# Order of the first loads, the token weight in three tiles, and the order of the first token products in a fused attention and mixer kernel

## Chip, cores and metric

The kernel runs on one core of one Trainium2 chip. The metric is the device time of one execution in microseconds (us); the median of several runs counts.

## What is computed

An attention block without softmax, normalised per head, is followed by an MLP mixer over tokens and then over channels. B = 8 batches, H = 8 heads, S = 576 tokens, D = 64, so d_model = 512; the token hidden size is 256, the channel hidden size 1536. All is float32.

```python
kv = np.einsum('bhsd,bhse->bhde', k, v)
out = np.einsum('bhsd,bhde->bhse', q, kv)
rms = np.sqrt(np.mean(out * out, axis=-1, keepdims=True) + 1e-06)
x = (out / rms * g_norm)            # (B,H,S,D) -> (B, S, H*D)
xt = x.transpose(0, 2, 1)
h = np.maximum(xt @ w_tok1, 0.0) @ w_tok2
u = x + h.transpose(0, 2, 1)
h2 = np.maximum(u @ w_ch1, 0.0) @ w_ch2
return u + h2
```

The four mixer weights arrive as 64-bit floats; the kernel reads them as pairs of 32-bit words and rounds them to 32-bit floats itself.

## The kernel before

Attention and token mixing go over the batches in pairs; the channel mixing of all batches follows and takes most of the time. The change is in the first pair and in the first third of the second ("the start" and "the middle").

**Loads.** `load(n)` (lines 138 to 147) fetches half the heads of one batch's k and v: for each, a DMA for tokens 0 to 511 and one for the last 64. The halves are numbered 0 to 15, and four tiles of each kind are used in turn. k goes on the SP queue, v too, except that v of halves 0 and 1 goes on ACT's queue. `load_q(b)` (149) fetches one batch's q without its last 64 tokens (1 MB), `load_q_rest` these. `block` (189) makes five steps for a part of a weight: step 0 fetches the raw words, step 1 (ScalarE, two instructions: the scaled value into the weight's tile, and the low word in place), step 2 (VectorE, clamp), step 3 (VectorE, shift), step 4 (VectorE, add of the low word). `get_tok1(t)` (204) is for half t of the first token weight, tokens 0 to 511, `get_tok1_rem` (210) for its last 64 tokens, `get_tok2(t)` (214) for the second token weight. The first token weight is one tile `w_tok1` [128, 5, 256] (101). The order of the first fetches is written out from line 1212 on; POOL there only sets padding rows and the identity.

**Order of the rest.** It is written out by hand as lists of step names (`start`, `middle`, `steady`, from line 1242), which `play` (1193) calls one by one. Every engine runs its own instructions in the order in which they are issued (`keep`, 118), and waits for the data. The names, for the first pair: `kv<s><h>` multiplies k and v of batch side s, half h, and `e<s><h>` copies the product out of PSUM (VectorE for side 0 of the first pair, ScalarE else). `a<c><t>` multiplies q with it for token tile c, half t (`a40`: the last 64 tokens of both sides). `g` (VectorE) multiplies with the gain, `q` (ScalarE) squares, `t` (VectorE) sums the squares, `m` (VectorE), `r` (ScalarE) and `i` (VectorE, four instructions) turn a tile's sums into factors. The factor is applied by ScalarE (`s<c><t>`, eight instructions) or by VectorE (`d<c><t>`, one). Tile c of side 0 is 0 or 1, of side 1 is 2 or 3, so the x tiles 0 to 7 are (c, t) in order. `h<s><t>` multiplies weight half t with the four x tiles of side s, `h<s><t><j>` with one of them; `hr` adds the last 64 tokens and takes the relu; `z` and `u` are the second token product. `w<n><k>` is step k of token weight part n (0 and 1 the halves of the first weight, 2 its last 64 tokens, 3 and 4 the second weight). `l`, `lq` and `lr` issue the next loads of k with v, q, and q's rest; `f` fetches a raw channel weight. `j<n>` (`keep_warm`, 1277) is n products of the identity with itself that nothing reads.

PSUM has two banks for attention (`o`), two for the k/v products (`kv`) and four for token products and junk (`h`).

Of the kernel before, what the change touches and what calls it, by code (L numbers as in the profile page):

```python
# [11 lines left out]
F32 = mybir.dt.float32  # L12
# [8 lines left out]
def kernel(  # L21
# [33 lines left out]
    P = 128  # L55
# [3 lines left out]
    DTOK = moe_w_tok1.shape[1]  # L59
    DCH = moe_w_ch1.shape[1]  # L60
    J, JJ, HF = 4, 5, 64
    LO = P * J
    assert D == 64 and DM == 512 and S == LO + HF and B % 2 == 0
    NC, NF, NTOK = DM // P, DCH // P, DTOK // P
# [13 lines left out]
    def pool(name, bufs, side="left", stack=ctx, **kw):  # L78
        return stack.enter_context(tc.tile_pool(name=name, bufs=bufs, side=side,
                                                reuse_waits="tile", **kw))  # L80
# [6 lines left out]
    tokw = pool("tokw", 1, "right", right)  # L87
# [10 lines left out]

    ident = inp.tile([P, P], F32, name="ident")
    g_sb = inp.tile([P, 1, D], F32, name="g_sb")  # L100
    w_tok1 = tokw.tile([P, JJ, DTOK], F32, name="w_tok1")
    w_tok2 = tokw.tile([P, NTOK, S], F32, name="w_tok2")

    w_ch1 = w1p.tile([P, 4, 4, FQ], F32, name="w_ch1")
# [7 lines left out]
    def do(f, *a, **kw):  # L112
        return lambda: f(*a, **kw)
# [6 lines left out]
    def dma(o, i, engine=nc.sync):  # L120
        keep(engine.dma_start(o, i))

    def tensor_add(o, a, b, op=ALU.add, engine=nc.vector):
        keep(engine.tensor_tensor(out=o, in0=a, in1=b, op=op))  # L124

    def relu(o, a):
        keep(nc.scalar.activation(o, a, AF.Relu))  # L127

    def copy(o, a):
        keep(nc.scalar.copy(o, a))  # L130

    def matmul(*a, **kw):
        keep(nc.tensor.matmul(*a, **kw))  # L133
# [4 lines left out]
    def load(n):  # L138

        if n >= 2 * B:  # L140
            return
        cols = [t[n // 2, :, ts(n % 2, DH)] for t in (k, v)]

        queues = (nc.sync, nc.scalar if n < 2 else nc.sync)
        for dst, c, e in zip((k_in[n % 4], v_in[n % 4]), cols, queues):
            dma(dst[:, :J], c[:LO].rearrange("(j p) e -> p j e", p=P), e)
            dma(dst[:HF, J], c[LO:], e)

    def load_q(b):
        if b < B:  # L150
            qT[b] = qtp.tile([P, HP, LO], F32, name="qT", tag="qT", bufs=2)
            dma(qT[b], q[b].rearrange("(c p) s -> p c s", p=P)[..., :LO])
# [29 lines left out]
    def words(w):  # L182
        return w.bitcast(U32).rearrange("r (n w) -> r n w", w=2)
# [5 lines left out]
    def block(n, loads, dst):  # L189

        raw = []

        def fetch():
            raw.append(stage.tile([P, n, 2], U32, name="raw", tag="raw", bufs=4))
            for o, i in loads(raw[0]):
                dma(o, i)

        def turn():
            t = raw[0]
            return t if len(dst.shape) == 2 else t.rearrange("p (a n) w -> p a n w", a=dst.shape[1])  # L200

        return (fetch,) + decode(dst, turn, lambda: raw[0])

    def get_tok1(t):

        rows = words(moe_w_tok1)[:LO].rearrange("(j p) n w -> p j n w", p=P)
        return block(J * P, lambda raw: [(raw.rearrange("p (j n) w -> p j n w", j=J),
                                          rows[:, :, ts(t, P)])], w_tok1[:, :J, ts(t, P)])

    def get_tok1_rem():  # L210
        w = words(moe_w_tok1)[LO:]
        return block(DTOK, lambda raw: [(raw[:HF], w), (raw[HF:], w)], w_tok1[:, J])

    def get_tok2(t):
        return block(S, lambda raw: [(raw, words(moe_w_tok2)[ts(t, P)])], w_tok2[:, t])
# [36 lines left out]
    def t_sums(b):  # L252

        def step(o, x, y):
            return lambda: tensor_add(b(o), b(x), b(y), ALU.subtract)

        return [step(5, 7, 1), step(6, 3, 5), step(7, 3, 7), step(4, 2, 6)]
# [92 lines left out]
    def x_of(pair, i):  # L350

        return X[pair, i // 2][:, i % 2]
# [177 lines left out]
    def token_mixing(pair, seeds, aside=()):  # L530
        h1, acc = {}, {}

        def tok1(side, t, js=range(J)):
            if js[0] == 0:
                acc[side, t] = ps["h"].tile([P, DM], F32, name="ps_h", tag="h")
            for j in js:
                matmul(acc[side, t], lhsT=w_tok1[:, j, ts(t, P)],
                                 rhs=x_of(pair, side * J + j), start=(j == 0), stop=False)

        def tok1_rem():  # L540
            for t in range(NTOK):
                for side in range(2):
                    r = ds(side * HF, HF)
                    matmul(acc[side, t], lhsT=w_tok1[r, J, ts(t, P)],
                                     rhs=x_of(pair, 8)[r], start=False, stop=True)
            for side in range(2):
                h1[side] = hp_.tile([P, NTOK, DM], F32, name="h1", tag="h1")
                for t in range(NTOK):
                    relu(h1[side][:, t], acc[side, t])

        def seed(i):


            acc[i] = ps["h"].tile([P, DM], F32, name="ps_u", tag="h")
            copy(acc[i], x_of(pair, i))

        def tok2(i):
            if i not in seeds:
                n = "o" if i in aside else "h"
                acc[i] = ps[n].tile([P, DM], F32, name="ps_u", tag=n)  # L560
            first = i not in seeds
            if i < 8:
                for t in range(NTOK):
                    matmul(acc[i], lhsT=w_tok2[:, t, ts(i % J, P)], rhs=h1[i // J][:, t],
                           start=(first and t == 0), stop=(t == NTOK - 1), skip_group_check=True)
            else:
                for t in range(NTOK):
                    for side in range(2):
                        matmul(acc[i][ds(side * HF, HF)], lhsT=w_tok2[:, t, LO:],
                               rhs=h1[side][:, t],  # L570
                               start=(first and t == 0), stop=(t == NTOK - 1), skip_group_check=True)
            x = x_of(pair, i)
            if first:
                tensor_add(x, acc[i], x)
            else:
                copy(x, acc[i])
            if i == 8:
                dma(u_rest[ts(pair, P)], x, nc.gpsimd)
                for side in range(2):
                    dma(out[2 * pair + side, LO:], x[ds(side * HF, HF)], nc.gpsimd)  # L580
            elif i % 2 == 1:
                dma(
                    u_rows(2 * pair + i // J)[ds((i % J - 1) * P, 2 * P)]
                    .rearrange("(t p) e -> p t e", p=P), X[pair, i // 2], nc.gpsimd)

        steps = {f"h{s}{t}": do(tok1, s, t) for s in range(2) for t in range(NTOK)}
        steps |= {f"h0{t}{j}": do(tok1, 0, t, (j,)) for t in range(NTOK) for j in range(J)}
        steps |= {f"z{i}": do(seed, i) for i in seeds}
        return steps | {"hr": tok1_rem} | {f"u{i}": do(tok2, i) for i in range(9)}

# [602 lines left out]
    def play(lines, after={}, **stages):  # L1193
# [3 lines left out]
        for name in " ".join(lines).split():  # L1197
# [5 lines left out]
            else:  # L1203
                next(stages[s][name] for s in ("attention", "mixing", "more")
                     if name in stages.get(s, ()))()


    tok1 = [get_tok1(t) for t in range(NTOK)] + [get_tok1_rem()]
    tok2 = [get_tok2(t) for t in range(NTOK)]
    channel = ([get_ch1(c, f) for f in range(2) for c in range(NC)]  # L1210
               + [get_ch2(f) for f in range(NF // 2)])
    load(0)
    for block in tok1[:2]:
        block[0]()
    load(1)
    for t in [t for pair in zip(k_in, v_in) for t in pair]:
        keep(nc.gpsimd.memset(t[HF:, J], 0.0))
    zeroed = [ps["kv"].tile([P, 2, P], F32, name="ps_kv", tag="kv") for _ in range(2)]
    for t in zeroed:
# [5 lines left out]
    make_identity(nc, ident)  # L1225
    dma(g_sb, bass.AP(tensor=g_norm.tensor, offset=g_norm.offset,
                      ap=[[0, P], [0, 1], list(g_norm.ap[0])]), nc.scalar)
    load_q(0)
    for n in range(2, 4):
        load(n)  # L1230
    load_q(1)
# [2 lines left out]
    for block in tok1[2:] + tok2:  # L1234
# [5 lines left out]


    start = [
        "kv00 e00 l00 j14 w01 w11 w02 w03 w04 w12 w13 w14", "kv01 j10 e01 l01",
        "a00 g00 q00", "a01 g01 q01 t00 t01 m0", "a10 q10 r0 i0 d00 d01", "a11 q11 g10 g11 t10",
        "kv10 e10 t11 m1 r1", "h000 h010 h001", "kv11 e11 i1 d10 s11", "h011", "a20 q20",
        "a21 q21 g20 g21 t20 t21 m2", "h002 h012 r2 i2 d20", "a30 q30 g30", "a31 q31 s21 g31 t30", "h003 h013 t31 m3",
        "a40 q40 r3 i3 d30 s31 g40 t40 m4 r4 w21 i4 s40 lq0 l10 l11 lr0 lr1"]
    middle = [
        "kv00 e00 w31 w22 w23 w24", "h10 -lq1 w32 w33 w34", "h11 w41 w42 w43 w44", "kv01 e01", "hr l00 z2",
        "a0 q00 g01 q01 g00 t00 t01", "u0 l01 f0", "u1 z4", "u2", "a1 q10 g11 q11 g10",  # L1250
        "kv10 kv11 e10 e11 t10 t11 m0 r0 lq0", "u3 z6 i0 d00 s01 d11 f1", "u4 l10", "a2 q20 g21 q21 g20",
        "a4 q40 t20 g41 q41 t21 g40 lr0 lr1", "u5 s10 t40 t41 m2 r2 f2 1", "u6 1 i2 p20 p21 l11 x00", "u7 1 1"]
# [17 lines left out]
    more = {f"w{n}{k}": f for n, b in enumerate(tok1 + tok2) for k, f in enumerate(b)}  # L1270
# [6 lines left out]
    def keep_warm(n):  # L1277

        o = ps["h"].tile([P, DM], F32, name="ps_j", tag="h")
        for _ in range(n):  # L1280
            matmul(o[:, :P], lhsT=ident, rhs=ident, start=True, stop=True)

    more |= {f"j{n}": do(keep_warm, n) for n in (10, 14)}
    play(start, attention=attentions[0], mixing=mixings[0], more=more)
    play(middle, attention=attentions[1], mixing=mixings[0], before=attentions[0],
         more=more, rounding=rounding)
    for n in range(1, B // 2 - 1):
        play(steady[n - 1], attention=attentions[n + 1], mixing=mixings[n], before=attentions[n] | {"u8": mixings[n - 1]["u8"]},
             more=more, rounding=rounding)
# [16 lines left out]
    more = {f"c{i}": f for i, f in enumerate(t_sums(lambda n: uT[0][:, SB[n]]))}  # L1306
# [97 lines left out]
```

## Time and profile before

| | us |
|---|---|
| median of 3 runs | 783.54 (783.22 to 783.66) |
| the profiled execution | 783.41 |
| its span, first to last instruction | 781.6 |
| TensorE busy in the span | 769.3 (98%) |
| VectorE busy | 617.4 (79%) |
| ScalarE busy | 271.1 (35%) |
| GpSimd busy | 70.5 (9%) |
| DMA, mean over the span | 246 GB/s |

The span is read from the start of the first instruction to the end of the last. PE is TensorE, DVE VectorE, ACT ScalarE, POOL GpSimd, and SP the engine that issues most DMAs. Matmuls run in a pipeline, so a busy TensorE is not one at its peak; a float32 product is two instructions in the trace. In a row of the timeline stand its start, its length, the engine and line, the operation with its tiles, the shape, the number of instructions, and in brackets the idle time ahead of it with what ended it. That releaser is inferred from semaphores: where an instruction waits for several things, it can be the wrong one.

### The profile page before, as it was taken

The numbers are of one execution on the slowest core, as the hardware profiler recorded it, in microseconds if no ns is written. First come the engines' busy times: TensorE is split into PE (matmuls) and PEld (weight loads), VectorE is DVE, ScalarE is ACT, GpSimd is POOL, SyncE is SP. The second block draws the span as 40 slices with busy tenths as digits, with TensorE's granted clock in tenths as the row PEclk, the third lists the DMA queues.
The fourth block names the chain that finished last, engine by engine and source line by source line (L and its number), as shares of the span: only waits on it lengthen the run. The fifth ranks groups of instructions, "written<-read, shape, count | busy, mean of one in ns | idle before, by whom it ended". The sixth has DMA issues, their size and how long they took to land.

```text
span 781.6 us, 14842 instructions
## 1 busy us (share of the span) xinstructions
PE 769.3 (98%) x5816; PEld 650.6 (83%) x5816; DVE 617.4 (79%) x924; ACT 271.1 (35%) x534; POOL 70.5 (9%) x84
## 2 busy tenths in 40 slices
PE   6999999999999999999999999999999999999998
PEld 5655555545888888999988899998889999889998
DVE  2867887897767779898768888876898885787977
ACT  2576565664210232511144241123352114325211
POOL 1002020113410000010100001010000101000111
PEclk9999999999999999999999999999999999999999
DMA  9999999599699795698996579889559889645864
GB/s 296 322 326 375 361 360 346 199 301 355 252 281 342 267 315 145 178 291 231 221 262 202 159 235 250 249 203 287 158 151 300 197 221 236 198 145 159 197 169 92
DMA packets 132613, 192.12 MB, mean 246 GB/s; under 512 B 13632, under 2 KB 92224, under 8 KB 132544
## 3 DMA queue, kind: packets, MB, share of 16 engines
q1 hardware_dynamic: 115984, 167.54, 68.1%
q0 software_dynamic: 14656, 22.02, 13.7%
q10 hardware_dynamic: 1904, 1.61, 0.7%
q8 instruction: 46, 0.75, 0.4%
q14 instruction: 23, 0.19, 0.1%
HBM read 138.31 MB, written 52.82 MB: 245 GB/s over the span
## 4 chain that ended last, share of the span: by engine, by line
PE 96%; DVE 1%; DMA 1%; ACT 1%; SPq 0%; issue 0%; ACTq 0%
PE ps_d L133 28%; PE ps_b L133 19%; PE ps_a L133 19%; PE ps_u L133 8%; PE ps_h L133 7%; PE ps_v L133 5%; PE ps_c L133 3%; PE ps_o L133 2%; PE ps_kv L133 2%; PE ps_w L133 2%; DMA raw<-in_moe_w_tok_dram 1%; DVE x L445 0%; PE ps_j L133 0%; DVE ms L466 0%; ACT x L499 0%; ACT sq L449 0%
## 5 line engine op out<-in xcount | busy, mean ns | idle before, releaser
L133 PE MATMUL ps_d<-ui,w 128*128 128x256 f32 x504 | 118.7, 379 | 0.0
L130 ACT COPY ps_d<-ps_a 128x768 f32<-128x768 f32 (+1 forms) x56 | 32.0, 571 | 215.3 <-PE ps_a L133 215.3
L133 PEld LDWEIGHTS ps_d<-ui,w 128*128 128x128 f32 x504 | 95.1, 190 | 12.9 <-DVE v L124 0.3
L124 DVE TENSOR_TENSOR v<-v,v 128x1536 f32<-128x1536 f32 (+2 forms) x70 | 103.4, 1482 | 0.3
L133 PE MATMUL ps_b<-w,sv 128*128 128x128 f32 x672 | 84.6, 276 | 0.0
L133 PE MATMUL ps_a<-w,v 128*128 128x128 f32 x672 | 84.2, 275 | 0.0
L133 PEld LDWEIGHTS ps_a<-w,v 128*128 128x128 f32 x672 | 79.8, 192 | 0.2
L133 PEld LDWEIGHTS ps_b<-w,sv 128*128 128x128 f32 x672 | 79.5, 192 | 0.2
L133 PE MATMUL ps_d<-w,v 128*128 128x128 f32 x528 | 66.2, 275 | 0.0
L133 PE MATMUL ps_h<-x,w_tok 128*128 128x512 f32 (+1 forms) x160 | 65.4, 603 | 0.6 <-DVE x L503 0.4
L133 PE MATMUL ps_u<-h,w_tok 128*128 128x512 f32 (+1 forms) x160 | 64.7, 599 | 0.0
L133 PEld LDWEIGHTS ps_d<-w,v 128*128 128x128 f32 x528 | 62.7, 192 | 0.3
L127 ACT ACTIVATE v<-v 128x768 f32<-128x768 f32 (+1 forms) x54 | 42.6, 821 | 55.1 <-DVE v L124 55.1
L133 PE MATMUL ps_d<-w,sv 128*128 128x128 f32 x480 | 60.1, 275 | 0.0
L133 PEld LDWEIGHTS ps_d<-w,sv 128*128 128x128 f32 x480 | 57.1, 192 | 0.2
L133 PEld LDWEIGHTS ps_h<-x,w_tok 128*128 128x128 f32 (+1 forms) x160 | 26.2, 189 | 32.3 <-issue 27.8
L133 PEld LDWEIGHTS ps_u<-h,w_tok 128*128 128x128 f32 (+1 forms) x160 | 25.6, 179 | 31.1 <-issue 26.7
L1122 POOL DMA_DIRECT2D out_dram<-us x11 | 14.2, 1292 | 379.5 <-ACT us L130 198.6
L133 PE MATMUL ps_a<-uT,w 128*128 128x256 f32 x192 | 46.7, 379 | 0.0
L133 PE MATMUL ps_b<-ui,w 128*128 128x256 f32 x168 | 40.8, 379 | 0.0
L133 PEld LDWEIGHTS ps_a<-uT,w 128*128 128x128 f32 x192 | 36.3, 190 | 4.8
L124 DVE TENSOR_TENSOR v<-ps_b,u 128x768 f32<-128x768 f32 x28 | 26.7, 954 | 15.3 <-PE ps_b L133 14.8
(145 smaller groups left out, 1207.0 us busy)
## 6 DMA issues: line engine op xcount, KB each, us to landing
w<-parts SPq DMA_DIRECT2D x168, 384.0 KB, 3.9
w<-parts SPq DMA_DIRECT2D x56, 192.0 KB, 3.3
uT<-blocks SPq DMA_DIRECT2D x36, 256.0 KB, 5.8
k_in<-in_k_dram SPq DMA_DIRECT2D x16, 512.0 KB, 8.9
qT<-in_q_dram SPq DMA_DIRECT2D x8, 1024.0 KB, 9.6
out_dram<-x POOLq DMA_DIRECT2D x16, 512.0 KB, 6.9
v_in<-in_v_dram SPq DMA_DIRECT2D x14, 512.0 KB, 9.2
raw<-in_moe_w_ch_dram SPq DMA_DIRECT2D x8, 768.0 KB, 8.7
```

Of the source, the lines that this page charges most:

```text
L124: keep(engine.tensor_tensor(out=o, in0=a, in1=b, op=op))
L127: keep(nc.scalar.activation(o, a, AF.Relu))
L130: keep(nc.scalar.copy(o, a))
L133: keep(nc.tensor.matmul(*a, **kw))
L1122: keep(nc.gpsimd.dma_start(to.rearrange("t p e -> p t e"), a, accum_op=ALU.add))
```

## The change

On SP the order of the first fetches becomes k of halves 0 and 1, q of the first batch, and then the two raw halves of the first token weight; before, these stood between the two k halves, and q behind both. The first token weight becomes three tiles of the same total size. The junk products j14 and j10 ahead of the first attention tile become j6 and j8, and a j12 is put ahead of the first token product. The decode steps of the first token weight move behind the attention tile a01. Of the factors, x tile 1 is now scaled by ScalarE (s01 for d01) and x tile 3 by VectorE (d11 for s11). The first token products are put in another order. In the middle, the token products of side 1 come one x tile at a time for both weight halves, ahead of kv00 and kv01 of the second pair, which stood before and after them; the decode steps w22 to w44 are spread anew.

```diff
-    w_tok1 = tokw.tile([P, JJ, DTOK], F32, name="w_tok1")
+    w_tok1 = [tokw.tile([P, J, P], F32, name=f"w_tok1{t}") for t in range(NTOK)]
+    w_tok1r = tokw.tile([P, DTOK], F32, name="w_tok1r")
...
-                                          rows[:, :, ts(t, P)])], w_tok1[:, :J, ts(t, P)])
+                                          rows[:, :, ts(t, P)])], w_tok1[t])
...
-        return block(DTOK, lambda raw: [(raw[:HF], w), (raw[HF:], w)], w_tok1[:, J])
+        return block(DTOK, lambda raw: [(raw[:HF], w), (raw[HF:], w)], w_tok1r)
...
-                matmul(acc[side, t], lhsT=w_tok1[:, j, ts(t, P)],
+                matmul(acc[side, t], lhsT=w_tok1[t][:, j],
...
-                    matmul(acc[side, t], lhsT=w_tok1[r, J, ts(t, P)],
+                    matmul(acc[side, t], lhsT=w_tok1r[r, ts(t, P)],
...
-        steps |= {f"h0{t}{j}": do(tok1, 0, t, (j,)) for t in range(NTOK) for j in range(J)}
+        steps |= {f"h{s}{t}{j}": do(tok1, s, t, (j,)) for s in range(2) for t in range(NTOK) for j in range(J)}
...
     load(0)
+    load(1)
+    load_q(0)
     for block in tok1[:2]:
         block[0]()
-    load(1)
...
-    load_q(0)
...
     start = [
-        "kv00 e00 l00 j14 w01 w11 w02 w03 w04 w12 w13 w14", "kv01 j10 e01 l01",
-        "a00 g00 q00", "a01 g01 q01 t00 t01 m0", "a10 q10 r0 i0 d00 d01", "a11 q11 g10 g11 t10",
-        "kv10 e10 t11 m1 r1", "h000 h010 h001", "kv11 e11 i1 d10 s11", "h011", "a20 q20",
-        "a21 q21 g20 g21 t20 t21 m2", "h002 h012 r2 i2 d20", "a30 q30 g30", "a31 q31 s21 g31 t30", "h003 h013 t31 m3",
+        "kv00 e00 l00 j6", "kv01 e01 l01 j8", "a00 g00 q00", "a01 g01 q01 t00 t01 m0 w01",
+        "a10 w02 w03 r0 w11 i0 d00 w04 q10", "a11 q11 s01 w12 w13 w14 j12", "h000", "kv10 e10 g10 g11 t10 t11 m1 r1",
+        "h001 h010 h011", "kv11 e11 i1 d10 d11", "a20 q20", "a21 q21 g20 g21 t20 t21 m2", "h002 h012 r2 i2 d20",
+        "a30 q30 g30", "a31 q31 s21 g31 t30", "h003 h013 t31 m3",
         "a40 q40 r3 i3 d30 s31 g40 t40 m4 r4 w21 i4 s40 lq0 l10 l11 lr0 lr1"]
     middle = [
-        "kv00 e00 w31 w22 w23 w24", "h10 -lq1 w32 w33 w34", "h11 w41 w42 w43 w44", "kv01 e01", "hr l00 z2",
+        "h100 h110 h101 h111 -lq1 w31 w22 w23 w24 w32", "h102 h112 h103 h113 w33 w34 w41 w42",
+        "kv00 kv01 e00 e01 w43 w44", "hr l00 z2",
...
-    more |= {f"j{n}": do(keep_warm, n) for n in (10, 14)}
+    more |= {f"j{n}": do(keep_warm, n) for n in (6, 8, 12)}
```

## The prediction, made before the result was known

> **What bounds the kernel now.** I read the page first, then the chain of waits, then the first 50 us by stretch and by instruction.
>
> ```profile
> PE   6999999999999999999999999999999999999998
> DMA  9999999599699795698996579889559889645864
> ```
>
> The first row is TensorE by fortieths of the span (19.5 us each). Only the first slice is not full, so work taken off TensorE's path in the first 20 to 50 us is worth its length, and nothing later is touched. The DMA row is full in that stretch too: a second bound to watch.
>
> ```profile
> core 0: us, PE busy (x) PEld busy (x) DVE busy (x) ACT busy (x) POOL busy (x), PEclk, DMA share, GB/s
> 0.00:17.61 17.61, 9.91 (x128) 9.59 (x129) 4.54 (x11) 3.96 (x6) 2.76 (x14) 1.00 0.93 294
> 17.61:28.92 11.31, 10.37 (x122) 7.66 (x121) 9.03 (x21) 4.04 (x11) 0.00 (x0) 1.00 1.11 309
> 28.92:36.30 7.38, 7.17 (x41) 4.91 (x40) 5.00 (x13) 5.05 (x18) 0.00 (x0) 1.00 1.07 343
> 36.30:47.38 11.08, 10.94 (x112) 6.23 (x112) 8.08 (x23) 8.99 (x29) 0.00 (x0) 1.00 1.09 333
> 47.38:100.00 52.62, 52.48 (x757) 29.29 (x754) 40.36 (x89) 30.42 (x74) 6.88 (x9) 1.00 1.07 356
> ```
>
> TensorE lacks 7.7 us before 17.61, 1.06 in the next stretch, then 0.2 and 0.1; after 47.38 it is full. DMA runs at about 310 to 350 GB/s throughout. The chain of waits names the places:
>
> ```profile
> 2.48 9.40 DMA raw<-in_moe_w_tok_dram
> ...
> 13.96 1.39 PE ps_kv L133 x40
> 15.35 2.43 PE ps_j L133 x20
> 17.78 0.91 PE ps_o L133 x8
> ...
> 39.51 2.03 ACT x L499 x8
> 41.58 4.56 PE ps_h L133 x10
> ```
>
> Columns are start and length. The second k/v product (kv01) starts at 13.96. The chain hangs it on the token-weight decode, but the DMA view shows another gate:
>
> ```profile
> k_in<-in_k_dram SPq DMA_DIRECT2D x1, 512.0 KB, 7.9
> qT<-in_q_dram SPq DMA_DIRECT2D x1, 1024.0 KB, 9.7
> raw<-in_moe_w_tok_dram SPq DMA_DIRECT2D x1, 512.0 KB, 9.4
> ```
>
> The last number is issue to landing. SP issues the second k at 5.96 (landed 13.9), q at 7.10 (16.8) and the second raw token weight at 2.48 (11.9). So k waits behind 1 MB of raw weights, q behind both. Ten junk products (x20) follow on the path, then the first attention tile (a00) at 17.61.
>
> ```profile
> 22.07 1.39 PE L133 MATMUL ps_kv<-v_in,k_in 128*64 128x64 f32 x40
> 26.64 1.39 PE L133 MATMUL ps_kv<-v_in,k_in 128*64 128x64 f32 x40
> 28.92 1.95 PE L133 MATMUL ps_o<-kvp,qT 128*128 128x128 f32 x16
> 36.30 1.09 PE L133 MATMUL ps_r<-kvp,qR 128*64 128x128 f32 x16 [0.21 <-DVE x L445]
> 37.29 1.39 PE L133 MATMUL ps_kv<-v_in,k_in 128*64 128x64 f32 x40
> 38.60 7.54 PE L133 MATMUL ps_h<-x,w_tok 128*128 128x512 f32 x16
> 46.07 1.39 PE L133 MATMUL ps_kv<-v_in,k_in 128*64 128x64 f32 x40
> 47.38 1.99 PE L133 MATMUL ps_h<-x,w_tok 64*128 64x512 f32 x8
> ```
>
> These are kv10, kv11, a20, a40, kv00 of the second pair, h10 with h11, kv01, and hr. Spacing of starts gives prices: a k/v product 1.31 us (37.29 to 38.60), a40 0.99. The h10/h11 stretch took 7.47 us.
>
> [...] ACT's and SP's loads together make the 294 GB/s of the first stretch. [...] junk starts are 0.207 us apart until 9.57, 3.5 us after the first product, then 0.111. [...]
>
> **The change, part by part.**
>
> *Queue order on SP.* Now k0, k1, q0, token weights 0 and 1 (two DMAs each for k). ACT's v loads and g_norm, and POOL's memsets, have the same order as before. In the trace a ninth outstanding DMA waits for an earlier landing (SP issues at 5.96 after v landed at 5.94, at 10.63 after the next v at 10.61), so about eight are in flight: q can be issued at 5.96, the weights at 6.6 and 7.2, all before the 1.2 MB of k and v ahead has drained. k1 takes the place of token weight 0, of equal size, which landed at 9.5; v1 landed at 10.6 and its remainder at 11.1. So kv01 starts at **10.7**, not 13.96, and ends at 12.0. The bytes up to the last of these five loads are the same set as before, which ended with q at 16.8. Backwards from there at 335 KB/us (estimate from the GB/s above): token weight 1 lands at 16.8, weight 0 at 15.2, q at 13.6. Everything queued behind (k2, v2, k3, v3, q1 and later) has the same bytes ahead, so it lands when it did: v3 at 25.2, q1 (issued 18.46, 9.6 to landing) at 28.04.
>
> *Junk.* j14 was off the path; j6 (12 instructions) ends by about 10.3 and hides under the wait for v1. j10 (x20, 15.28 to 17.61, 0.1165 each) becomes j8: 1.86. a00 starts at 12.0 + 1.86 = **13.9**, above q's 13.6; with 0.05 of slack, 13.95: 3.66 earlier. But j12 is new: 24 x 0.1165 = 2.8 us, on the path between a11 and h000. "Fewer" holds only for the early ones: 26 products for 24.
>
> *Decode moved behind a01 (w01 to w14).* It costs nothing where it was removed (ACT and VectorE were idle for it), and now gates h000. From a00 at 13.95, with before's offsets (g00 at +1.10, m0 done at +4.24): q01 ends 17.27, m0 18.19. ACT: w01 takes 1.26 (before, 9.49 to 10.75) to 18.54; r0 to 18.77; w11 to 20.0. VectorE: w02 and w03 0.46 each to 19.11, i0 1.0 to 20.1, d00 0.69 to 20.8, w04 0.69 to **21.5**. Meanwhile a11 ends at 18.4 and j12 at 21.2. So h000 starts at 21.58, 0.4 of it idle. Queued behind on ACT: q10, q11, then s01 (eight activations, 2.02) to 23.3; on VectorE: w12 to w14 to 23.3, then g10. h001 needs s01, h010 needs w14, both after 23.7. Making the token weight three tiles changes no instruction; it only frees h000 from weights it doesn't read.
>
> *From h000 to a20.* h000 0.92 (0.86 and a restart), kv10 1.33, h001, h010, h011 2.57 (1.72 per four instructions, 30.71 to 32.43), kv11 1.32: kv11 ends 27.7. No product is left between kv11 and a20 to cover the eviction e11 (0.37), so a20 starts at 28.25; q1's landing at 28.04 would not let it start before 28.1. Before: 28.92. Gain **0.67**. Exchanging s11 for d11 costs VectorE 0.65, when it is waiting (d11 ends by 28.7, g20 needs a20 at 29.2), and frees q20.
>
> *From a20 to a40* the chain through g, t, m2, i2, d20, g30 is the same, so a40 keeps the 0.67: 35.6.
>
> *Second batch by x tile.* Eight products, each 2 x 0.43 = 0.86: 6.86 us if none waits. x tiles 6 and 7 (d30, s31; before ready at 40.2 and 41.54, now about 39.6 and 40.9) are needed at 40.0 and 41.7 instead of right at the start. The 7.47 becomes 6.86: gain **0.61**. kv00 and kv01 move behind; their v landed at 37.6 and 41.3, so kv00 no longer leans on a landing (before, 37.29 for 37.15). Evictions e00, e01 now queue behind w31 and w41 on ACT, to about 47.1, in time for a0 at 48. The k loads that reuse their tiles are issued from 48.49 on, later than kv00's end at 44.8, so SP is not held. hr: 36.6 + 6.86 + 2.6 = **46.1** against 47.38.
>
> *After hr* nothing changes and TensorE never idles. ACT waits for raw channel weights at 87.1 (0.3) and 132.3 (3.1). If those land no earlier, 1.3 more is covered by the 3.1 us that ACT then waits for h, and by the 2.4 us from the second relu's end (135.5) to the product that reads it (137.9). The gain stays.
>
> **Sum:** 0.67 + 0.61 = 1.28 us. The profiled execution took 783.41 (span 781.6); less 1.28 is 782.13. The median is 783.54, 0.13 above the profiled one, so **782.2**. The bounds of the unknown sizes: a20 at 28.1 to 28.9 (landings of v1 and q1, each known to about 0.3, and the ACT/VectorE walk), h10/h11 gain 0.3 to 0.7.
>
> **Rivals.** About 0.2% (1.57 us) is what a measurement of this kernel can tell from no change.
> (a) *Decode and e11 cost less*: if w04 comes with j12 and a20 lands at q1's limit or q1 lands sooner, TensorE's own work bounds it: 0.4 of idle before h000 and 0.2 at a40 go too. Gain 1.9: **781.6**. For: j12 ends just where w04 does. Against: q1's landing.
> (b) *The load bound holds*: q or v1 lands 0.7 us later than I place it, a20 keeps its time, and only the reordering pays: **782.9**. For: DMA is full. Against: the sets of bytes are equal.
> (c) *Slower: a cold clock.* j6 is shorter, so TensorE may rest before kv01; if the clock is not yet released, or is lost, kv01 costs 1.0 more (kv00 took 2.33) and j8 16 x 0.096 = 1.5 more. a00, h000 and a20 come 2.5 later; a20 1.9 later than before, less 0.61: **784.8**. It decides once h000 starts over 1.3 us late, after 22.9; a decode held by a token weight landing after 18.5 would do the same. Against: the clock was released at 9.57 under six junk products, and the gap of 1.7 us before 13.96 didn't take it away.
>
> **Chances.** Forecast (within 0.2%) 0.52, (a) 0.25, (b) 0.10, (c) 0.13. So faster 0.25, same 0.62, slower 0.13. The range 781.4 to 783.5 reaches over (a) and (b) and leaves out (c).
>
> **What would show it.** kv01 at 10.7, a00 at 13.9, h000 at 21.5, a20 at 28.2, hr at 46.1. VectorE, not junk, released h000; an ACT eviction released a20. If a00 is not over 3 us earlier, the order of loads did not do it; if h10/h11 still takes over 7.2 us, the tile order did not; if hr is early and the end is not, a later wait took it.

## Result, and the profile after

The changed kernel takes **786.06 us** (median of 15 runs, 784.68 to 788.04); the kernel before, run beside it, takes 783.54 (median of 15, 782.92 to 785.14). The ratio is 1.0031, with an interval of 1.0022 to 1.004: slower by 2.5 us, where the prediction said 1.3 us faster. The profiled execution took 786.15 (span 784.4), 2.74 more than the one before.

The slices of the page hardly differ; first TensorE's row, then DMA's.

```profile
PE   6999999999999999999999999999999999999998
DMA  9999999589699795598896579889559889655864
```

The stretches that were shown of before, in the kernel after (same columns):

```profile
0.00:17.61 17.61, 10.97 (x129) 10.41 (x130) 3.25 (x8) 2.47 (x4) 2.76 (x14) 1.00 0.91 292
17.61:28.92 11.31, 10.63 (x125) 7.76 (x123) 10.02 (x25) 6.42 (x19) 0.00 (x0) 1.00 1.12 295
28.92:36.30 7.38, 7.03 (x40) 5.01 (x40) 4.51 (x11) 3.30 (x9) 0.00 (x0) 1.00 1.07 319
36.30:47.38 11.08, 10.87 (x115) 6.30 (x114) 8.21 (x23) 8.99 (x30) 0.00 (x0) 1.00 1.10 314
47.38:100.00 52.62, 50.79 (x749) 28.53 (x750) 39.10 (x84) 30.80 (x75) 6.88 (x9) 1.00 1.07 355
```

TensorE's busy time up to 47.38 is about what it was (39.50 for 38.39 us, with some of it junk). What is new is the last row: 50.79 of 52.62, where before had 52.48. The stretch in which the prediction saw nothing change has lost 1.7 us. TensorE's timeline shows where, and how the start went:

```profile
11.31 1.39 PE L134 MATMUL ps_kv<-v_in,k_in 128*64 128x64 f32 x40
...
14.51 1.95 PE L134 MATMUL ps_o<-kvp,qT 128*128 128x128 f32 x16
...
21.79 1.13 PE L134 MATMUL ps_h<-x,w_tok 128*128 128x512 f32 x2
...
29.27 2.02 PE L134 MATMUL ps_o<-kvp,qT 128*128 128x128 f32 x16 [0.95 <-DMA qT<-in_q_dram]
...
37.76 7.13 PE L134 MATMUL ps_h<-x,w_tok 128*128 128x512 f32 x16
44.82 2.55 PE L134 MATMUL ps_kv<-v_in,k_in 128*64 128x64 f32 x80
47.30 1.99 PE L134 MATMUL ps_h<-x,w_tok1r 64*128 64x512 f32 x8
49.22 1.14 PE L134 MATMUL ps_o<-kvp,qT 64*64 64x64 f32 x59
52.19 0.34 PE L134 MATMUL ps_o<-kvp,qT 64*64 64x64 f32 x5 [1.83 <-issue]
52.45 4.13 PE L134 MATMUL ps_u<-h,w_tok 128*128 128x512 f32 x9
```

These are kv01, a00, h000, a20, h1 by x tile, kv00 with kv01 of the second pair, hr, a0 in two rows, and the first nine of the twelve products of u0 to u2. Two rows matter. a20 waits 0.95 us for the second batch's q. And a0 stops after 59 of its 64 matmul instructions for 1.83 us, with "issue" as releaser: no semaphore, no engine and no load that the profile shows. The chain of waits has both on it:

```profile
10.43 9.24 DMA k_in<-in_k_dram
...
19.68 9.46 DMA qT<-in_q_dram
...
49.29 1.07 PE ps_o L134 x59
50.36 1.83 issue
52.19 0.34 PE ps_o L134 x5
```

Set beside before, instruction by instruction: a00 is 3.1 us earlier (14.51 for 17.61), a20 0.35 later (29.27 for 28.92), hr 0.08 earlier (47.30 for 47.38), u0 2.06 later (52.45 for 50.39). A short stop of before at 64.6 us is gone (-0.35), a wait for ScalarE's x at 165 is new (+0.32), and this at 283:

```profile
283.04 2.21 PE L134 MATMUL ps_d<-ui,w 128*128 128x256 f32 x9 [0.62 <-DVE v L125]
```

It shifts what follows by 0.72. The sum, 2.06 - 0.35 + 0.32 + 0.72 = 2.75, is the difference of the two executions.

### The profile page after: what moved, and what is told of

Read it like the earlier page. It is cut to its first block, busy times and chain, and to the rows that moved or that the text cites. A ratio compares the mean times of both kernels' runs of the same rounds, so it can differ in the third digit from the quotient of the medians.

```text
span 784.4 us, 14850 instructions
## 1 busy us (share of the span) xinstructions
PE 770.7 (98%) x5820; PEld 651.6 (83%) x5820; DVE 617.4 (79%) x924; ACT 270.5 (34%) x534; POOL 70.8 (9%) x84
## 4 chain that ended last, share of the span: by engine, by line
PE 87%; DMA 6%; DVE 3%; ACT 2%; issue 1%; SPq 0%; ACTq 0%; DVEq 0%
PE ps_d L134 28%; PE ps_b L134 18%; PE ps_a L134 18%; PE ps_u L134 6%; PE ps_v L134 5%; PE ps_h L134 4%; PE ps_c L134 3%; PE ps_w L134 2%; DMA v_in<-in_v_dram 2%; PE ps_kv L134 2%; PE ps_o L134 1%; DMA qT<-in_q_dram 1%; DMA k_in<-in_k_dram 1%; DMA raw<-in_moe_w_ch_dram 1%; DMA xt<-out_dram 1%
## 5 line engine op out<-in xcount | busy, mean ns | idle before, releaser
L134 PE MATMUL ps_h<-x,w_tok 128*128 128x512 f32 x128 | 57.7, 600 | 0.1
L134 PEld LDWEIGHTS ps_h<-x,w_tok 128*128 128x128 f32 x128 | 23.4, 190 | 27.8 <-issue 24.2
L446 DVE TENSOR_TENSOR x<-ps_o,g_sb 128x512 f32<-128x512 f32 x32 | 21.2, 686 | 23.2 <-PE ps_o L134 14.4
```

Source lines behind the costliest of these rows:

```text
L446: keep(nc.vector.tensor_mul(x, bank[c, h], g_sb.to_broadcast([P, number(c), D])))
```

## Theories

**Instructions run out** (theory F in the expectations below)**.** Of the queues that carry instructions the page lists as the larger:

```profile
q8 instruction: 46, 0.75, 0.4%
```

46 packets and 0.75 MB make 16 KB each. The page lists 5820 matmul instructions and as many weight loads for TensorE, which is 253 for each packet. The theory takes this queue for TensorE's own and a packet for a block of its instructions. The last of the 46 packets came at 767.0 us, with 123 of the 5820 matmul instructions still to run, 246 with their weight loads: about what one packet carries, so there the fetch was about one block ahead. By these numbers a block holds some 127 matmul instructions with their weight loads (an estimate: half of 253). Counted backwards from the stop: 59 of a0, 8 of hr and 60 of the 80 of kv00 and kv01. By this count that block began with the twenty-first of the 80, at 44.82 + 20 x 0.031 = 45.4, and was used up at 50.36: 4.9 us. Before, with kv00 far ahead and four junk instructions fewer, the 127 that end at the same place (63 of a0, 8 of hr, 40 of kv01, 16 of h10 and h11) begin at 38.6 and last 11.8 us. The theory: kv00 moved behind the token products packs a block into less time than the fetch of the next one takes. The next fetch shows in the DMA view of 49.0 to 50.5 us:

```profile
q1 hardware_dynamic: 496, 0.44, 106.1%
q8 instruction: 1, 0.02, 4.8%
```

4.8% of 16 engines x 1.5 us is 1.15 us for one packet, begun at 49.39, some 4 us after the block began, and over at 50.5. TensorE restarts 1.65 us after that; what fills this time the trace does not show. From 45.4 to the restart at 52.19 are some 6.7 us (an estimate, since the count marks the start).

**q lands late** (theory L)**.** The second batch's q, placed at 28.04 as before, came at 19.68 + 9.46 = 29.14. Its time in transit was about the 9.6 us of before; its issue was late. In both traces SP issues it 0.02 us after the third load of k has landed, at 19.66 here and at 18.44 before.

**Rivals.** That the start alone costs the time (late q, cold clock), and the stop in a0 is a shadow of something that ScalarE or VectorE does; that later waits (165, 280 us) belong to the number of instructions; that the new load order itself is at fault.

## Experiments

Each ratio is against the kernel before, run beside it, whose median was 783.25 to 783.5 in all of them; an interval stands in brackets. The ratio is not exactly the quotient of the two medians.

**1. Each half alone.** The changed kernel with the middle of before (new_start), and the kernel before with the middle of the change (new_middle):

```diff
 new_start
-        "h100 h110 h101 h111 -lq1 w31 w22 w23 w24 w32", "h102 h112 h103 h113 w33 w34 w41 w42",
-        "kv00 kv01 e00 e01 w43 w44", "hr l00 z2",
+        "kv00 e00 w31 w22 w23 w24", "h10 -lq1 w32 w33 w34", "h11 w41 w42 w43 w44", "kv01 e01", "hr l00 z2",
 new_middle: the same lines, the other way, in the kernel before
```

> The changed kernel's first stage (loads, junk, decode, order up to a40) with the middle of the kernel before. Theory F (TensorE runs out of instructions in a0, because the two k/v products of the second pair now stand together just ahead of it): no stall of over 0.3 us in a0; a40 keeps or loses a few tenths, h10/h11 takes about 7.5 us again; time within 0.8 us of before (782.7 to 784.3). Theory L (the new order of loads makes q1 and what follows land about 1 us later, and that is carried to the end): q1 lands at about 29.1 again, a20 starts at 29.3, and the time is 1 us or more over before (784.5 to 786).

> The kernel before with the changed middle alone (token products of side 1 by x tile, kv00 and kv01 together behind them). Theory F: a stall of 1.5 to 2 us in or near a0, h10/h11 0.5 us shorter; time 784.3 to 785.5, slower than before by about 1.3. Theory L: no stall that matters, 0.5 us gained in h10/h11; time 782.7 to 783.2.

new_start: 784.21, ratio 1.0012 [1.0003, 1.0022], a0 in one piece. new_middle: 784.5, ratio 1.0013 [1.0005, 1.0022], and the stop is there, with the start of before:

```profile
44.92 2.55 PE L133 MATMUL ps_kv<-v_in,k_in 128*64 128x64 f32 x80
47.40 1.99 PE L133 MATMUL ps_h<-x,w_tok 64*128 64x512 f32 x8
49.32 1.16 PE L133 MATMUL ps_o<-kvp,qT 64*64 64x64 f32 x63
52.39 0.27 PE L133 MATMUL ps_o<-kvp,qT 64*64 64x64 f32 x1 [1.92 <-issue]
```

So the middle brings the stop, not the start. It comes after 63 instructions, not 59. The junk of before's start is 48 instructions, the new one's 52: four fewer ahead, and the stop four later. A wait for data would stay with its product; this place is counted in instructions: in both kernels, and in the second execution of the changed one below, 471 matmul instructions of TensorE lie ahead of it.

The stop is not the whole loss. By the medians each half alone is about 1 us slower than before (784.21 and 784.5 for 783.4), where the prediction gave the start a gain of 0.67 and the middle one of 0.61. In the start it is the second batch's q: in new_start's trace a20 begins at 29.97, after 2.03 us of waiting for it.

**2. kv00 behind two token products instead of eight.** The changed kernel with kv00 behind those of the first x tile:

```diff
-        "h100 h110 h101 h111 -lq1 w31 w22 w23 w24 w32", "h102 h112 h103 h113 w33 w34 w41 w42",
-        "kv00 kv01 e00 e01 w43 w44", "hr l00 z2",
+        "h100 h110 kv00 e00 h101 h111 -lq1 w31 w22 w23 w24 w32", "h102 h112 h103 h113 w33 w34 w41 w42",
+        "kv01 e01 w43 w44", "hr l00 z2",
```

> The changed kernel with kv00 and e00 moved between the first and the second x tile of side 1, so that only 40 short k/v instructions stand just ahead of a0 and not 80. Theory F: the fetch of the next block of instructions starts about 5 us earlier, the stall of 1.83 us in a0 goes to under 0.3; time 783.5 to 784.7, 1.5 us or more under the changed kernel. Theory L: the stall may go, but the end stays within 0.5 us of the changed kernel, because later loads decide.

784.36, ratio 1.0011 [1.0004, 1.0019]; the same number of instructions, and no stop:

```profile
45.51 1.39 PE L134 MATMUL ps_kv<-v_in,k_in 128*64 128x64 f32 x40
46.82 1.99 PE L134 MATMUL ps_h<-x,w_tok1r 64*128 64x512 f32 x8
48.74 1.16 PE L134 MATMUL ps_o<-kvp,qT 64*64 64x64 f32 x64
49.83 4.99 PE L134 MATMUL ps_u<-h,w_tok 128*128 128x512 f32 x11
```

u0 is at 49.83, 2.6 us earlier than in the changed kernel and 0.56 earlier than before. Of the 2.6, 0.48 were there at hr: its start is the same code as the changed kernel's, but a20 came at 28.44, with the idle time of 0.95 gone, because q landed at 28.31. The gain was then lost at 280 us, where ps_d waited 0.88 for VectorE's v.

**3. The changed kernel again, unchanged.**

> The changed kernel, once more, for a second trace. Both theories: 785 to 787. Theory F: the stall in a0 is there again, between 1 and 3 us, and most of the spread of its times is the spread of this stall. Theory L: q1 lands at 28.8 or later again, and the DMA rate between 18 and 50 us is 3% or more under that of before.

785.58, ratio 1.0029 [1.0019, 1.004]. In another execution the stop is at the same instruction, at another time:

```profile
50.44 1.14 PE L134 MATMUL ps_o<-kvp,qT 64*64 64x64 f32 x59
53.27 0.34 PE L134 MATMUL ps_o<-kvp,qT 64*64 64x64 f32 x5 [1.69 <-issue]
```

The wait at 280 us is not there: the same kernel has it in one execution and not in another.

**4. The middle as it is, fewer instructions ahead of it.** Without j12 (24 fewer), and with j12 as three products of the identity with 512 columns of q, as long but 18 instructions fewer:

```diff
 no_j12
-        ... "a11 q11 s01 w12 w13 w14 j12", "h000",
+        ... "a11 q11 s01 w12 w13 w14", "h000",
 wide_junk: "wide" for "j12", with
+        o = ps["h"].tile([P, DM], F32, name="ps_j", tag="h")
+        for i in range(3):
+            matmul(o, lhsT=ident, rhs=qT[0][:, i], start=True, stop=True)
```

> The changed kernel without the twelve junk products ahead of the first token product; everything else, the middle too, stays. That is 48 TensorE instructions fewer ahead of the second pair[...]. Theory F: the point where the instructions run out moves from inside a0 into the long second-stage products behind it, and the stall of 1.7 to 1.8 us in a0 is gone although the order of the middle is unchanged; time 783.6 to 784.6. Rival G (the two k/v products together, or a0 behind them, are slow by themselves, whatever the block): the stall stays, time 785 to 786. On the junk: if q1's landing gates a20, a20 starts within 0.3 us of where it did (22.5 to 23.6 us after the first product); if the junk was on the path, a20 starts up to 1 us earlier. If TensorE's clock falls in the pause that the junk filled, kv10 takes over 2 us and the time is 786 or more.

> The changed kernel, its middle kept, with j12 replaced by three junk products of 512 columns (the identity with q): 6 x 0.43 = 2.6 us of work for 2.8, but 36 TensorE instructions fewer. Theory F: no stall in a0 although kv00 and kv01 stand together; the clock is kept, as with j12. Time: the fast half of the runs of the kernel without j12 (782.8 to 783.8), with a20 gated by q1 at 21.8 to 23.5 us after the first product. Rival: the stall stays, 785 to 786.

no_j12: 784.22, ratio 1.0004 [0.9995, 1.0013]. wide_junk: 783.7, ratio 1.0006 [0.9997, 1.0016]. Both keep kv00 and kv01 side by side in front of hr, and a0 runs through. Of wide_junk:

```profile
44.57 2.55 PE L134 MATMUL ps_kv<-v_in,k_in 128*64 128x64 f32 x80
47.05 1.99 PE L134 MATMUL ps_h<-x,w_tok1r 64*128 64x512 f32 x8
48.97 1.16 PE L134 MATMUL ps_o<-kvp,qT 64*64 64x64 f32 x64
50.06 4.99 PE L134 MATMUL ps_u<-h,w_tok 128*128 128x512 f32 x11
```

By the count the block now ends 18 later, at the start of a1, behind the twelve products of u0 to u2, which take 0.43 us each: it lasts some 5 us longer. With experiment 1 this settles what places the stop: not the order of the work by itself, but where the short matmul instructions fall by the count.

The kernel before has the same thing in small. Its stop at 64.6 us stands behind 723 matmul instructions, 252 behind the place of the large one:

```profile
64.59 0.21 PEld L133 LDWEIGHTS ps_r<-kvp,qR 64*64 64x64 f32 x8 [0.28 <-issue]
```

In six other traces (before_again, new_middle, early_j10, new_start, kv00_early, old_loads) the step behind the same 723 is 0.07 to 0.10 us long where its neighbours take 0.06 or less, and in the last three of these another product stands there. In new_middle, which has both places, the trace lists 511 TensorE instructions from the one to the other, weight loads and waits among them: some 255 for each of two blocks, close to the 253 of a packet. The 127 matmul instructions that end there take 6.0 us in the trace of before (58.28 to 64.3), so that was about the limit here.

no_j12 shows what j12 is for:

```profile
21.38 1.13 PE L134 MATMUL ps_h<-x,w_tok 128*128 128x512 f32 x2 [2.76 <-DVE w_tok L179]
...
29.65 2.02 PE L134 MATMUL ps_o<-kvp,qT 128*128 128x128 f32 x16 [1.74 <-DMA qT<-in_q_dram]
```

Here the decode lets h000 go at 21.38, with a00 at 14.04. In the changed kernel's profiled run, where a00 came at 14.51, j12 ends at 21.71 and the decode at 21.74, so j12 costs nothing on the path; it fills a gap of 2.8 us. Nine of 14 runs of no_j12 had a mean granted clock under 0.999.

**5. The order of the loads.** kv00_early with the SP order of before:

```diff
 load(0)
-load(1)
-load_q(0)
 for block in tok1[:2]:
     block[0]()
+load(1)
+load_q(0)
```

> The changed kernel with kv00 early, and the first loads on SP in the order of the kernel before (k0, token weights, k1, q0). If the new order of loads is what lets the first stage end on time: kv01 starts at about 14, a00 at 17 to 17.5, h000 at about 25, a20 at 31 to 32, time 786.3 to 788. If the loads were no gain at all because q1 gates a20 in either order (theory L in its strong form): a20 at 28.5 to 29.5 and the time within 0.5 us of the kernel with kv00 early.

787.14, ratio 1.004 [1.003, 1.005], 2.8 us over kv00_early.

```profile
14.46 1.97 PE L134 MATMUL ps_kv<-v_in,k_in 128*64 128x64 f32 x40 [2.42 <-issue]
16.36 3.02 PE L134 MATMUL ps_j<-ident 128*128 128x128 f32 x16
19.22 1.95 PE L134 MATMUL ps_o<-kvp,qT 128*128 128x128 f32 x16
```

kv01 is back at 14.46 (k, as in before; the row's "issue" names nothing) and after 2.4 us without work TensorE is slow: kv01 1.97 for 1.39, j8 3.02 for 2.05. a00 is 4.7 us later than in kv00_early (3.7 counted from the first product). About 1.5 us of this is the slower products (0.58 of kv01, 0.97 of j8), in an execution whose mean granted clock was 0.998; a00 was expected at 17 to 17.5 and came at 19.22. The clock is not the whole: of the six runs with a mean granted clock of 1.0 three took 784.7 to 785.2 and three 787.4 to 787.6, and what divides them is not shown. So the load order as such is not at fault: it pays for the decode's move behind a01.

**6. Without j12 and with kv00 early; the kernel before again.**

> The changed kernel with kv00 between the first and second x tile, and without j12: both reliefs together. Theory F: no stall in a0 in either; the time is that of the kernel with kv00 early (784.4 median), within 0.5 us, since q1 gates a20 and the junk lay in the time that TensorE waits for q1 anyway. If the junk was on the path: 783.6 or less, faster than with kv00 early by 0.7 us or more.

> The kernel before, once more, for a second trace. Time 783 to 784, ratio 0.999 to 1.001. q1's first part lands about 20.1 us after the start of the first product, as in every run; its last part 21.5 to 22.2 if the lag of the slowest DMA engine belongs to the old order, up to 23.5 if it comes and goes with the run.

early_no_j12: 784.17, ratio 1.0007 [1.0, 1.0014]; a gap of 2.76 before h000 and, in the profiled run, h000 1.81 for 1.13 at a clock of 0.998. No better than either edit alone. before_again: 783.22, ratio 0.9996 [0.9988, 1.0004]: what one kernel differs from itself.

**7. The number of instructions and the later waits.** kv00_early with j10 for j12 (four fewer), and the kernel before with j16 for j14 (four more, the changed kernel's number):

> The changed kernel with kv00 early and with ten junk products for twelve, so that TensorE has as many instructions ahead of every later point as the kernel before. Theory P (where the ends of the instruction blocks fall decides the small losses too: with four products more, the fetch near 280 us starts 1.7 us earlier in the program and holds back the load of x that VectorE transposes there): no idle of over 0.3 us near 280 (0.9 with kv00 early), no stall in a0, time 0.5 to 1.0 us under the kernel with kv00 early: 783.2 to 783.9. Rival (chance of the single run): the idle near 280 is there in this trace as in three of five traces with four products more, time 784.0 to 784.6.

> The kernel before with two junk products more (j16 for j14), which end by about 13 us, before kv01 can start: nothing on the path, but all later TensorE instructions stand eight further on, as in the changed kernel. Theory P: idle of 0.6 to 0.9 us near 280 and time up by 0.4 to 0.8 us (783.8 to 784.3). Rival: nothing changes, ratio 0.9995 to 1.0005.

early_j10: 783.84, ratio 1.0012 [1.0003, 1.0021]; nothing at 280 us, but 0.4 of idle at 137 and 0.3 at 165. before_j16: 783.47, ratio 1.0006 [0.9998, 1.0014], nothing at 280. The first is what the theory of the instruction number (P in the expectations) expected, the second is against it. One execution each decides nothing: of the five traces of changed kernels with that number (after, after_again, new_start, kv00_early, old_loads) two have no wait at 280 either. Whether the number matters there stays open.

**8. Both remedies.** wide_junk with kv00 early, behind the first two token products (one x tile, both weight halves; the expectation calls them two tiles).

> The changed kernel with two edits: the 24 small junk products ahead of the first token product are three products of the same length with 512 columns, and kv00 of the second pair stands behind the first two x tiles of h1 instead of beside kv01. Each edit alone took the stall out of a0. Theory (the stall is only a matter of how many short TensorE instructions follow one another, and what is left over is q's late landing): no stall in a0, hr between 46.3 and 47.1, u0 between 49.4 and 50.2, and the median between 783.0 and 783.6, equal to the kernel before. Rival (small idle stretches later in the program, at 165 and 280 us, give back whatever the start gains): u0 as early, but the median at 783.7 to 784.4, as in the kernel with kv00 early alone.

783.78, ratio 1.0006 [0.9996, 1.0016]. No stop in a0, but u0 only at 50.42, since the first product came at 6.85 (6.13 in the changed kernel's profile); then 0.3 of idle at 165. The two don't add up. The rival had the median, neither had u0. No version here is measurably faster than the kernel before.

## Why the prediction was wrong, point by point

**The step that failed most: "After hr nothing changes and TensorE never idles ... The gain stays."** The products after hr are the same, but the row of instructions ahead of them, by which the stop is placed, was not. The prediction moved kv00 behind the token products and priced it by its length alone. Measured: 1.83 us of stop in a0, 1.69 and 1.92 in two other executions of this middle with the same number of instructions ahead of the stop, none in the kernels in which the count lets the block last 9 us or more (kv00_early, no_j12, wide_junk). hr was at 47.30 for 47.38, u0 at 52.45 for 50.39: this step is 2.1 of the 2.7 us between the two profiled executions. That a fetch of instructions ends these stops is inferred from the count and the packets; that the place goes by the count is shown.

**The term that was mis-sized: a20.** Predicted 28.25, measured 29.27; so the 0.67 became -0.35. The term for q was "issued 18.46, 9.6 to landing"; the 9.6 held (9.46) and the issue did not (19.68). "Everything queued behind has the same bytes ahead, so it lands when it did" was the prediction's estimate, and off already for the third load of k, on which that issue waits. Of its sixteen parts the median landed 11.70 us after the first product, 11.69 before; the last one at 13.54 for 12.41. Of q's sixteen parts the median landed 20.90 us after the first product, 20.49 before; the last one at 23.01 for 22.01, and a20 needs the last. Over the executions:

| counted from the first product, us | issue of q | last part landed |
|---|---|---|
| old load order, five traces | 12.06 (11.84 to 12.43) | 21.9 (21.5 to 22.3) |
| new load order, nine traces | 13.22 (12.57 to 13.79) | 22.5 (21.3 to 23.5) |

The issue is 0.01 or 0.02 us after k's last part in all fourteen. So with equal bytes ahead the median parts moved by 0.01 us for k and 0.41 for q, the last ones by 1.13 and 1.00. A packet of TensorE instructions, 1.14 us long, came at 16.0 us here and at 18.5 before: in the nine traces 2.9 to 5.1 us ahead of k's last part, in the five within 0.3 us of it. That it holds up k's last part is a guess from these times; it was not shown. kv00_early, with the same start, had a20 at 28.44: with q in time, the predicted 28.25 holds to 0.2.

**Right: the first loads.** kv01 at 11.31 (10.7), a00 at 14.51 (13.9), "over 3 us earlier"; old_loads takes it away again. The 0.6 is j6: said to end by 10.3 and to hide, it ran at about half speed (2.92 us for 12 instructions, 2.05 for j8's 16) and ended at 11.3, on the path, because the clock was released at 11.23 and not at 9.57.

**Right: h000.** 21.79 for 21.58. "VectorE, not junk" holds, barely: the last decode step of VectorE ended at 21.74, j12 at 21.71.

```profile
21.05 0.69 DVE L179 CUSTOM_DVE_ANT_1 w_tok<-w_tok,raw 128x1024 uint16<-128x1024 uint16 x1
```

The 0.4 of idle ahead of h000 shrank to some 0.1: a00 came 0.6 late and the walk through ScalarE and VectorE from there took 0.3 less. The other sign, "an ACT eviction released a20", failed: the load of q did.

**Right in mechanism: tile order in the middle.** The eight products took 7.06 (37.76 to 44.82), predicted 6.86, before 7.47. A gain of 0.4, not 0.61.

**The rivals.** (c) alone foresaw a slower kernel, 784.8 for the 786.06 measured, and by the wrong cause: h000 was not late. Cold clocks did come, in other executions (below). (b) named a late q among its reasons, and was right on a20; it had not seen a0.

**Open.** Why the last part of q lags behind the fifteenth by 0.5 us in some executions and by over 2 in others, and what in the new order holds up the last part of k. What puts the small waits at 137, 165 and 280 us into one execution and not the next; in the profiled run those at 165 and 283 make 1.04 of the 2.74 us. And whether wide_junk, no_j12 and wide_kv00 are equal to the kernel before or slower by some 0.05%: their intervals hold both.

## What to carry to other kernels

An order of products has a second cost beside their lengths: count the instructions. Before putting many short matmuls in a row, see how long the TensorE instructions of one packet last there (253 by the count here, weight loads among them); here some 5 us was too short, 6 us was at the edge (a stop of 0.35 us in one execution, under 0.1 in six), 9 us or more was enough. When loads are reordered, look at the last part of a landing and not at its middle: here, with the same bytes ahead, q's median part came 0.4 us later, its last of sixteen 1.0, and a20 needed the last.

## What the runs showed of the hardware

- A row "<-issue" stood in the middle of a run of equal matmuls (1.83 us in the changed kernel, 1.69 in its second execution, 1.92 in new_middle), and moved four instructions on when four were taken away ahead of it. The packets point to the instruction fetch: in the traces of the changed kernel and of new_middle one of 1.15 us begins some 4 us after the counted start of the block (at 49.39 and at about 49.6), and TensorE goes on 1.6 us behind its end. The stop at 64.6 us in the kernel before was 0.35 us.
- TensorE slowed down after some gaps and not after others. After 2.03 us of idle in new_start a20 took 3.30 us for 2.02, in an execution whose mean granted clock was 0.998:

```profile
29.97 3.30 PE L134 MATMUL ps_o<-kvp,qT 128*128 128x128 f32 x16 [2.03 <-DMA qT<-in_q_dram]
33.06 2.29 PE L134 MATMUL ps_h<-x,w_tok 128*128 128x512 f32 x4
```

  After 2.42 us in old_loads kv01 took 1.97 for 1.39, and after 2.76 in early_no_j12 h000 took 1.81 for 1.13, both again with a mean of 0.998. After the same 2.76 in no_j12 h000 took 1.13, at a mean of 1.000, and after the 1.83 in a0 of the changed kernel nine products of u0 to u2 took 4.13, the same as nine in early_no_j12 without a stop. What decides between them is not shown.
- The spacing of the junk products halves, from 0.213 to 0.111 us, at 9.57 in the kernel before, 3.5 us after the first product. In the changed one j6's instructions stand 0.213 apart, and the record of the granted clock turns to full at 11.23, 5.1 us after the first product at 6.13. In early_no_j12, with the first product at 6.75, kv01 at 11.94 still took 1.81 for 1.39. So the time to the full clock differs from run to run.
